# Transpose copies of batch 0's queries exchanged between ScalarE and VectorE, and batch 1's second query transposed three matmuls later

One NeuronCore of one Trainium2 chip. The metric is the device time of one execution in microseconds (us), smaller is better.

## The reference

Linear attention over 8 batches, 8 heads, 576 positions of 64 features, followed by a gated feed-forward block over all 4608 tokens:

```python
q_s = exp(q - max(q, -1));  q_s = q_s / (sum(q_s, -1) + 1e-09)       # per position
k_s = exp(k - max(k, 2));   k_s = k_s / (sum(k_s, 2) + 1e-09)        # per feature
kv  = einsum('bhsd,bhse->bhde', k_s, v)
x   = einsum('bhsd,bhde->bhse', q_s, kv)     # then (b, s, h*d): 4608 x 512
g   = x @ w_gate                             # 512 -> 1536
out = (g * sigmoid(g) * (x @ w_val)) @ w_out # 1536 -> 512
```

## The kernel before

The feed-forward block fills TensorE for nearly the whole run; the attention of each batch is threaded in between. A batch has two groups G of four heads. For each, the query goes: exponential (`eq`, ScalarE), row sums and product with their reciprocals (`qs`, VectorE), nine 128x128 transposes on TensorE into two PSUM banks (`tp`), and a copy of each bank to SBUF (`qt`). The keys and values give `kv` on TensorE, which is normalised to `kn`; the product of `kn` and `qt` is `xp`, copied to `xt`, the feed-forward's input. From batch 2 on, the transposes run on the DMA queues; the change touches batches 0 and 1 alone.

```python
BANKS = ((0, 5), (5, T))                 # T = 9 blocks: 640 and 512 columns

def turn_pe(b, G, i):                    # transposes of one bank
    ...
    tp = s["tp", i] = psp.tile([128, 1024], BF16, tag="ps", name="tp")
    for t in range(t0, t1):
        nc.tensor.transpose(out=tp[...], in_=s["qs"][:, t, :], identity=ident)

def turn_out(b, G, i, eng):              # copy of one bank to qt, on eng
    ...
# ---- batch 0 (cut)
turn_out(0, 0, 0, nc.scalar)
exp_of("k", 0, 1)
turn_out(0, 0, 1, nc.scalar)
norm_mul(0, 1, BANKS)                    # qs of query 1, VectorE
spin(6)
kv_first(0)
key_sum(1)
scale_first(0, nc.scalar)                # kn of group 0
turn_pe(0, 1, 0)
turn_pe(0, 1, 1)
turn_out(0, 1, 0, nc.vector)
turn_out(0, 1, 1, nc.vector)
xp0 = x_mm(0, 0, 0), x_mm(0, 0, 1)       # the first product
kv_first(1, *BANKS[0])
kv_first(1, *BANKS[1])
x_out(0, 0, 0, xp0[0], (nc.scalar, None))
scale_first(1, nc.vector)                # kn of group 1: half ScalarE, half VectorE
x_out(0, 0, 0, xp0[0], (None, nc.vector))
x_out(0, 0, 1, xp0[1])
xp1 = x_mm(0, 1, 0), x_mm(0, 1, 1)       # the second product
# ---- batch 1 (cut); o_mm(j, ..., m0, m1) are output matmuls of row block j
i = norm_mul(1, 1)                       # qs of the second query, VectorE
cast_v(1, 0)                             # v to bf16, GpSimd
c = cast_v(1, 1)
...
o_mm(2, p2, m0=4)                        # eight matmuls
turn_out(1, 0, 1, nc.vector)
turn_pe(1, 1, 0)                         # the second transposes
turn_pe(1, 1, 1)
turn_out(1, 1, 0, nc.scalar)
turn_out(1, 1, 1, nc.vector)
st["kv", 1] = [bank("kv") for _ in range(2)]
p3 = o_mm(3, m1=6)                       # six matmuls
o_out(2, p2)
kv_both(1)
scale_both(1)                            # kn
exp_of("q", 2, 0)
o_mm(3, p3, m0=6, m1=11)                 # five, while kn is made
x_and_next_kv(1, with_kv=False)          # the product of batch 1
o_mm(3, p3, m0=11)                       # one, while xt is copied
```

The softmax here doesn't subtract the row's maximum and nothing guards it: scores larger than these inputs give would overflow.

## Time and profile before

| | before |
|---|---|
| time, median of 3 runs first, of 6 with those beside the changed kernel | 311.65, then 311.62 (311.32 to 311.97) |
| span in the profile | 309.74 |
| first output matmul | 37.755 |
| from there to kv of batch 1 | 10.363 |
| from there to the last TensorE instruction | 267.968 |

Three-decimal times are starts of single instructions, read from the trace in narrow windows. The page's shares and TensorE's waits stand in the prediction. The following rows are the timeline of the kernel before (start, duration, engine, line, operation, what it writes from what, shapes, count, and in brackets the idle time before it with what is taken to have ended it):

```profile
12.70 0.44 PE L202 MATMUL xp<-qt,kn 64*64 64x320 bf16 x8
...
13.47 0.31 ACT L420 ACTIVATE kn<-kv,kvr 128x64 bf16<-128x64 f32 x1
13.52 0.28 DVE L424 TENSOR_SCALAR kn<-kv,kvr 128x64 bf16<-128x64 f32 x1
...
13.84 0.45 PE L202 MATMUL xp<-qt,kn 64*64 64x320 bf16 x8 [0.42 <-DVE kn L424]
...
42.20 2.01 POOL L124 CAST vb<-v 128x1152 bf16<-128x1152 f32 x1 [20.27 <-DMA v<-in_v_dram]
44.80 1.36 DVE L149 TENSOR_TENSOR qs<-eq,rr 128x1152 bf16<-128x1152 bf16 x1
...
47.42 0.67 ACT L108 COPY qt<-tp 128x640 bf16<-128x640 bf16 x1
...
48.12 0.69 PEld L189 LDWEIGHTS <-ek 64*64 64x64 bf16 x72 [0.42 <-ACT qt L108]
```

### The profile page before, as it was taken

The page shows a single profiled execution, that of the slowest core. Times are in us where ns is not written, and L with a number is a line of the kernel's source. Part 1 is how long each engine was busy: PE and PEld are TensorE (multiplying, and loading weights), DVE is VectorE, ACT ScalarE, POOL GpSimd, SP SyncE. Part 2 cuts the span into 40 slices and gives each one's busy share as a digit, 9 for nine tenths or more (in the row PEclk, how much of TensorE's full clock was granted, in tenths as well). Part 3 has the DMA queues.
Part 4 walks back from the last instruction along what each step waited for, and adds up shares of the span by engine and source line. Part 5 has one row for each costly group of instructions (what it writes and reads, how often), then busy time and mean ns, then how long its engine had stood idle before and what let it go on. Part 6 is the DMA issues. An engine that isn't in the chain of part 4 may idle for free.

```text
span 309.7 us, 5467 instructions
## 1 busy us (share of the span) xinstructions
PE 302.8 (98%) x2182; PEld 150.3 (49%) x2182; DVE 161.9 (52%) x286; ACT 146.3 (47%) x214; POOL 32.8 (11%) x39
## 2 busy tenths in 40 slices
PE   6999999999999999999999999999999999999995
PEld 2688745554445444454445444544444444444443
DVE  3844477945754566365826492639353324433421
ACT  5843578785674375547464737455043113312300
POOL 2960021510200110002000200000000000000000
PEclk9999999999999999999999999999999999999999
DMA  7999999999347815590739352605310302020133
GB/s 273 189 195 207 275 389 389 349 219 389 79 87 200 327 33 114 135 382 13 144 74 353 102 121 61 186 0 107 72 35 0 70 11 56 3 68 8 26 71 103
DMA packets 43018, 45.78 MB, mean 148 GB/s; under 512 B 19568, under 2 KB 28272, under 8 KB 42992
## 3 DMA queue, kind: packets, MB, share of 16 engines
q1 hardware_dynamic: 34096, 39.95, 43.4%
q0 software_dynamic: 8752, 5.31, 12.0%
q8 instruction: 17, 0.28, 0.4%
q10 hardware_dynamic: 144, 0.16, 0.2%
q14 instruction: 9, 0.07, 0.1%
HBM read 37.75 MB, written 9.44 MB: 152 GB/s over the span
## 4 chain that ended last, share of the span: by engine, by line
PE 96%; DMA 1%; DVE 0%; ACT 0%; issue 0%
PE g_ps L284 30%; PE u_ps L284 30%; PE o_ps L317 29%; PE kv L189 2%; PE xp L245 1%; PE idle L388 1%; DMA q<-in_q_dram 1%; PE tp L164 1%; PE o_ps L338 1%; DVE rs L135 0%; PE xp L202 0%; PE kv L411 0%; ACT eq L121 0%; ACT xt L259 0%; PE ks L397 0%; DVE o_sb L342 0%
## 5 line engine op out<-in xcount | busy, mean ns | idle before, releaser
L291 ACT ACTIVATE sg<-g_ps 128x512 bf16<-128x512 f32 (+2 forms) x120 | 64.7, 554 | 133.6 <-PE g_ps L284 120.5
L293 DVE TENSOR_TENSOR hr<-sg,u_ps 128x512 bf16<-128x512 bf16 (+3 forms) x120 | 72.5, 616 | 86.3 <-PE u_ps L284 80.7
L284 PE MATMUL g_ps<-xt,wg 128*128 128x512 bf16 (+2 forms) x480 | 111.4, 358 | 0.1
L284 PE MATMUL u_ps<-xt,wv 128*128 128x512 bf16 (+2 forms) x480 | 111.3, 358 | 0.0
L317 PE MATMUL o_ps<-wo,hr 128*128 128x512 bf16 x420 | 93.9, 379 | 0.0
L284 PEld LDWEIGHTS <-wv 128*128 128x128 bf16 x480 | 46.9, 98 | 46.4
L284 PEld LDWEIGHTS <-wg 128*128 128x128 bf16 x480 | 46.3, 98 | 45.5 <-issue 0.6
L317 PEld LDWEIGHTS <-hr 128*128 128x128 bf16 x420 | 40.9, 98 | 48.6
L110 DVE COPY o_sb<-o_ps 128x512 f32<-128x512 f32 x33 | 22.4, 680 | 39.0 <-PE o_ps L317 39.0
L124 POOL CAST vb<-v 128x1152 bf16<-128x1152 f32 x14 | 17.8, 1277 | 135.8 <-DMA v<-in_v_dram 106.6
L135 DVE TENSOR_REDUCE rs<-eq 128x18 f32<-128x1152 bf16 (+2 forms) x18 | 21.7, 1213 | 12.7 <-ACT eq L121 12.7
L149 DVE TENSOR_TENSOR qs<-eq,rr 128x1152 bf16<-128x1152 bf16 (+2 forms) x18 | 22.1, 1234 | 0.1
L121 ACT ACTIVATE eq<-q 128x1152 bf16<-128x1152 f32 (+2 forms) x18 | 18.3, 1051 | 4.1 <-DMA q<-in_q_dram 4.0
L121 ACT ACTIVATE ek<-k 128x1152 bf16<-128x1152 f32 (+2 forms) x17 | 17.9, 1101 | 0.5 <-DMA k<-in_k_dram 0.5
L291 ACT ACT_TABLE_LOAD x12 | 15.4, 1283 | 0.2
L121 ACT ACT_TABLE_LOAD x11 | 14.1, 1283 | 0.2
L388 PE MATMUL idle<-zero 128*128 128x512 bf16 x20 | 7.9, 560 | 2.6 <-DVE rs L135 1.4
L259 ACT CAST xt<-xp 128x512 bf16<-128x512 f32 x14 | 7.8, 586 | 4.5 <-PE xp L245 4.5
L260 DVE CAST xt<-xp 128x512 bf16<-128x512 f32 x14 | 9.0, 683 | 0.7 <-PE xp L245 0.7
L189 PEld LDWEIGHTS <-ek 64*64 64x64 bf16 x504 | 6.3, 107 | 1.7 <-ACT qt L108 0.4
L189 PE MATMUL kv<-vb,ek 64*64 64x65 bf16 x504 | 6.7, 194 | 0.0
L245 PE MATMUL xp<-qt,kn 64*64 64x512 bf16 (+1 forms) x112 | 6.7, 292 | 0.0
(44 smaller groups left out, 67.4 us busy)
## 6 DMA issues: line engine op xcount, KB each, us to landing
q<-in_q_dram SPq DMA_DIRECT2D x16, 576.0 KB, 5.4
out_dram<-o_sb SPq DMA_DIRECT2D x70, 128.0 KB, 2.3
k<-in_k_dram SPq DMA_DIRECT2D x12, 576.0 KB, 7.2
v<-in_v_dram SPq DMA_DIRECT2D x12, 576.0 KB, 9.1
wo<-in_moe_w_out_dram POOLq DMA_DIRECT2D x4, 384.0 KB, 15.4
k<-in_k_dram SPq DMA_DIRECT2D x4, 320.0 KB, 8.2
k<-in_k_dram SPq DMA_DIRECT2D x4, 256.0 KB, 8.1
v<-in_v_dram SPq DMA_DIRECT2D x2, 320.0 KB, 6.9
```

The source lines that it names most:

```text
L110: eng.tensor_copy(out=out, in_=in_)
L121: nc.scalar.activation(out=e[:, t0:t1], in_=src[:, t0:t1], func=AF.Exp)
L124: return nc.gpsimd.tensor_copy(out=vbs[G][:, :, :, 0:64], in_=raw["v", b, G].rearrange("p h (t d) -> p t h d", d=64),)
L135: i = nc.vector.reduce_sum(out=rs[:, 2 * t0:2 * t1], in_=eq2[:, 2 * t0:2 * t1, :], axis=mybir.AxisListType.X)
L149: last = eng.tensor_mul(qs[:, t0:t1, :].rearrange("p t (h d) -> p (t h) d", d=64), eq2[:, 2 * t0:2 * t1, :], s["rr"][:, 2 * t0:2 * t1].to_ ...
L189: nc.tensor.matmul(out=kv[g][HALF[h], c:c + 65], lhsT=ek[HALF[g], t, h, :], rhs=vbs[G][HALF[g], t, h, :], start=(t == 0), stop=(t == T - 1),)
L245: nc.tensor.matmul(out=o[h][HALF[g], c:c + 64 * (t1 - t0)], lhsT=kn[HALF[h], g, G, :], rhs=qt[G][HALF[h], t0:t1, 64 * g:64 * g + 64], star ...
L284: nc.tensor.matmul(out=gu[a][i][:, 0:w_], lhsT=(wg, wv)[a][:, kk, ms], rhs=xt[:, kk, c:c + w_], start=(kk == 0), stop=(kk == KT - 1),)
L291: nc.scalar.activation(out=sg[:, 0:w_], in_=g_ps[:, 0:w_], func=AF.Silu)
L293: nc.vector.tensor_mul(hr[:, m, r:r + w1], sg[:, 0:w1], u_ps[:, 0:w1])
L317: nc.tensor.matmul(out=o_ps, lhsT=hr[:, m, r0:r0 + 128], rhs=wo[:, m, :], start=(m == 0), stop=(m == MT - 1),)
L388: i = nc.tensor.matmul(out=idle, lhsT=zero[:, 0:128], rhs=zero, start=True, stop=True)
```

## The change

The intent is to take a copy off ScalarE where kn of group 0 follows, to free VectorE's xp copy from waiting behind kn, and to keep TensorE busy while VectorE makes qs of batch 1's second query.

```diff
+    def turn_bank(b, G, i):
+        st[b, G]["tp", i] = psp.tile([128, 1024], BF16, tag="ps", name="tp")
     def turn_pe(b, G, i):
...
-        tp = s["tp", i] = psp.tile([128, 1024], BF16, tag="ps", name="tp")
+        if ("tp", i) not in s:
+            turn_bank(b, G, i)
+        tp = s["tp", i]
@@ batch 0
-        turn_out(0, 0, 1, nc.scalar)
         norm_mul(0, 1, BANKS)
+        turn_out(0, 0, 1, nc.vector)
...
-        turn_out(0, 1, 0, nc.vector)
+        turn_out(0, 1, 0, nc.scalar)
         turn_out(0, 1, 1, nc.vector)
...
-        x_out(0, 0, 0, xp0[0], (nc.scalar, None))
+        x_out(0, 0, 0, xp0[0])
         scale_first(1, nc.vector)
-        x_out(0, 0, 0, xp0[0], (None, nc.vector))
@@ batch 1
         turn_out(1, 0, 1, nc.vector)
+        for i in range(2):
+            turn_bank(1, 1, i)
+        st["kv", 1] = [bank("kv") for _ in range(2)]
+        p3 = o_mm(3, m1=3)
         turn_pe(1, 1, 0)
         turn_pe(1, 1, 1)
         turn_out(1, 1, 0, nc.scalar)
         turn_out(1, 1, 1, nc.vector)
-        st["kv", 1] = [bank("kv") for _ in range(2)]
-        p3 = o_mm(3, m1=6)
+        o_mm(3, p3, m0=3, m1=6)
```

## The prediction

> **What bounds the kernel now.** I read the page's busy shares first, then the chain that ended last, then TensorE's waits by window, and last the timeline of the two stretches that the change touches: the opening (0 to 17 us) and batch 1's attention between two feed-forward stages (42 to 60 us).
>
> From the page of the kernel before, the busy shares and the chain by line:
>
> ```profile
> PE 302.8 (98%) x2182; PEld 150.3 (49%) x2182; DVE 161.9 (52%) x286; ACT 146.3 (47%) x214; POOL 32.8 (11%) x39
> PE 96%; DMA 1%; DVE 0%; ACT 0%; issue 0%
> ```
>
> TensorE (PE) is the bound: 98% busy and 96% of the chain. VectorE (DVE) and ScalarE (ACT) are half idle, so moving a copy between them is worth only what it lets TensorE do sooner. What can be won is TensorE's idle time in the two stretches. Its waits from 0 to 17 us, complete:
>
> ```profile
> PE idle L388 <- DVE rs L135: 1.4, 1, 1.4
> PE idle L388 <- DVE sel L367: 1.2, 1, 1.2
> PE xp L202 <- DVE kn L424: 0.4, 1, 0.4
> ```
>
> The first two are start-up (loads, softmax sums) and untouched. The third is the wait of batch 0's second product (xp) for the normalised kv (kn). From 42 to 60 us the same view lists no wait at all, but that is an effect of modelled matmul ends. The weight-load row shows what the matmul row hides:
>
> ```profile
> 44.25 1.45 PEld L317 LDWEIGHTS <-hr 128*128 128x128 bf16 x8
> 46.21 0.17 PEld L164 LDWEIGHTS <-qs 128*128 128x128 bf16 x3 [0.52 <-DVE qs L149]
> ```
>
> The weights of batch 1's second transposes could not be loaded before the normalised query qs was written. The matmul rows around it:
>
> ```profile
> 44.30 1.89 PE L317 MATMUL o_ps<-wo,hr 128*128 128x512 bf16 x8
> 46.22 0.28 PE L164 MATMUL tp<-ident,qs 128*128 128x128 bf16 x2
> ```
>
> The eight output matmuls start 216 ns apart, the last at 45.81; TensorE is free for the next at 45.81 + 0.22 = 46.03. The transposes start at 46.22, just after qs is done (VectorE's product runs 44.80 to 46.16). So TensorE stands idle 46.22 - 46.03 = 0.19 us here. The 0.52 in brackets is not the stall: the weight loader always runs ahead and rests while the array streams.
>
> **What the Trainium skill says.** "TensorE: Matmul & The Clock Gate", section "Wait — 56ns, not 53.3ns?", gives 55.6 and 215.7 ns start to start for 128 and 512 columns at full clock. The trace agrees: 24 output matmuls hold the chain 5.18 us (216 ns each) and nine transposes plus the hand-over take 46.22 to 46.73 (57 ns each). "TensorEngine Tiling (Array Packing)", section "Key Properties", says that a change of tiling mode drains TensorE. The trace agrees with a gap: before the first 64x64 kv matmul at 48.12 the last output matmul (start 47.81) has been streamed at 48.03, so 0.09 us are lost; the same 0.08 appears at 58.78, 68.70 and 99.24. This matters, because the profile puts the gap at 48.12 down to ScalarE's copy of qt, which happens to end at 48.10; kv does not read qt, so I take that label for a coincidence. "ScalarE: Activation LUTs", section "What ACT_TABLE_LOAD costs", gives 186 ns + 0.833 ns per element for an ACTIVATE without pointer operands and an overlap of about 93 ns between neighbours: an estimate of 719 ns for 640 columns. The trace has 692 for that copy out of PSUM, so I use the trace. VectorE does the same 640-column bf16 copy in 491 ns and the 512-column one in 415, against ScalarE's 576.
>
> **Part A, the exchange in batch 0.** It takes two copies from one engine and puts them on the other: qt of query 0, second piece (512 columns), goes from ScalarE (576 ns) to VectorE (415); qt of query 1, first piece (640), goes from VectorE (491) to ScalarE (692). VectorE's copy of the first xp bank is put ahead of its kn, and no longer behind. TensorE's order is the same, so I follow each of its waits.
>
> First product (12.70): its last transpose starts at 12.55, ends its stream at 12.61, plus the mode change 0.09 makes 12.70. TensorE itself sets it. kn of query 0 is ready at 12.51 and the earlier qt piece will be ready at about 12.22 on VectorE (behind the product that ends at 11.88). Gain 0.
>
> Second product (13.84): kv of query 1 ends at 13.43. ScalarE's kn half runs 13.475 to 13.79, VectorE's 13.52 to 13.80, and TensorE starts 0.04 later. Now both halves have a copy in front:
> - ScalarE: the 640-column copy starts at 12.585 (when the fifth transpose is done, as VectorE's did), and gives way after 0.59 (its spacing in the trace from 9.784 to 10.372), at 13.17, to the first xp copy, which ran at 13.07 before. That one gives way after 0.32, at 13.495: kn 13.495 to 13.81, 0.02 later than before.
> - VectorE: the 512-column copy starts when the last transpose is done, 12.77 + 0.04 = 12.81, and gives way 0.33 later at 13.14; the xp copy of 320 columns then holds it for 0.40 (13.719 to 14.117 in the trace): 13.53. kn could start there, or some 0.05 later if its pointer operand again costs what lies between 13.43 + 0.04 and 13.52. So 13.53 to 13.59 against 13.52: 0.01 to 0.07 later.
> The second product slips by 0.02 to 0.07; I take 0.04. The xp copies that follow on VectorE come some 0.2 us earlier, but the first feed-forward matmuls, spaced 0.49 per four (2 x 320 + 2 x 256 columns), show no wait for them before, so that buys nothing. Part A: +0.04 us.
>
> **Part B, the later transposes in batch 1.** It moves three of the six output matmuls (m 0 to 2 of row block 3) from behind the nine transposes to ahead of them; no instruction is added. They fill the hole: start at 46.03 in place of 46.73, 3 x 0.216 = 0.65 later, at 46.68, the transposes start, and qs has been ready since 46.16. The hole of 0.19 closes. Then nine transposes 0.51 (47.19), three output matmuls 0.65 (47.84), mode change 0.09: kv at 47.93 in place of 48.12.
>
> Does anything stop kv from starting at 47.93? Its ek halves end on ScalarE at 46.37 and 47.52, its v casts on GpSimd at 47.37. The qt copies: VectorE's is set by the last transpose, 47.34 + 0.04 to 47.81 (0.45 later than before); ScalarE's starts at 47.43 behind the exponentials as before and ends at 48.10. The product that reads them comes at 50.04, or 49.85 now. VectorE must then empty row block 2 (0.68, to about 48.41) before it turns to kn at about 48.78. All have room. The hole before the first feed-forward matmul (streamed 50.88, start 51.13, waiting for ScalarE's xt copy) moves as a whole. Later, ScalarE works behind TensorE until about 59 us, yet the first banks needed again (at 57.2 and 57.9) were read by about 57.2; the transposes by DMA land at 67.2 and 68.2 for use at 68.70 and 69.25. 0.19 us fits. Part B: -0.19 us, which carries to the end, for TensorE shows no wait after 60 us.
>
> **Sum:** -0.19 + 0.04 = -0.15 us: 311.65 - 0.15 = 311.5.
>
> **Rivals.** (1) kv really waits for the qt copy on ScalarE, as the label at 48.12 says. Then kv stays at 48.12, part B gives 0 and the time is 311.7. For it: the label, and 48.10 + 0.03. Against: the data, and the same gap where no such copy runs. (2) kn becomes the bound in the opening: if VectorE can start kn only when the xp copy in front has ended (13.62), the second product slips by 0.15 to 0.2 and eats part B: 311.65. Against: the VectorE rows overlap by 0.08 throughout. (3) The exchange frees the opening: the copy that left ScalarE (11.44 to 12.02) lay right ahead of kn of query 0 (11.98), and an earlier kn would lead to 311.3. Against: kv ends only at 11.94, and TensorE's own transposes set 12.70. (4) Eight PSUM banks are handed out in order of release; the exchange changes that order, and a matmul could draw a bank that is read later. A wait of 0.2 to 0.5 would give 311.8 to 312.
>
> **Range and chances.** Every term is below 0.1% of the time; even both real holes together (0.42 + 0.19) are 0.6 us, and 2% is 6.2 us. The range holds rivals 1 to 3 and the smaller waits of rival 4, and the spread of the runs (0.22 us) with some more for another chip: 311.1 to 311.9. Faster or slower by over 2% could come only from something that no view shows: 0.005 each.
>
> **What would show it.** Right: three output matmuls ahead of the second transposes, whose weight loads wait for no VectorE product; kv of batch 1 0.15 to 0.19 earlier counted from the first output matmul at about 37.8; the second product of batch 0 at 13.85 to 13.91. Wrong: kv still just behind ScalarE's qt copy; a second product at 14.0 or later, or before 13.8; a new PE wait after 52 us.

## The result

The changed kernel takes 311.5 us (median of 6 runs, 311.21 to 311.76) against 311.62 for the kernel before in the same rounds (6 runs, 311.32 to 311.97). The ratio of the mean times of the runs of the same rounds is 0.9996, 95% interval 0.9983 to 1.0009; such ratios are of means of shared rounds, so not quite the ratio of the medians quoted. The times alone do not show even the sign. The traces show more.

From the page of the changed kernel, busy shares and chain:

```profile
PE 299.9 (97%) x2157; PEld 149.6 (48%) x2182; DVE 161.6 (52%) x286; ACT 146.4 (47%) x214; POOL 32.6 (11%) x39
PE 94%; DMA 2%; DVE 1%; issue 1%; ACT 1%; SPq 0%
```

The lower PE share is no loss of work: 2157 in place of 2182 matmul records, with 2182 weight loads in both, are missing records. TensorE's waits from 0 to 17 us in the changed kernel:

```profile
PE idle L393 <- DVE rs L135: 1.7, 1, 1.7
PE idle L393 <- DVE sel L372: 1.2, 1, 1.2
PE kv L416 <- DMA v<-in_v_dram: 0.7, 1, 0.7
PE xp L207 <- ACT kn L425: 0.4, 1, 0.4
PE tp L169 <- DVE qs L149: 0.2, 1, 0.2
```

The wait for kn is as long as before, and two others are there that belong to this execution's loads. The timeline of the changed kernel, the rows that answer to those of before:

```profile
12.63 0.44 PE L207 MATMUL xp<-qt,kn 64*64 64x320 bf16 x8
...
13.40 0.31 ACT L425 ACTIVATE kn<-kv,kvr 128x64 bf16<-128x64 f32 x1
13.47 0.28 DVE L429 TENSOR_SCALAR kn<-kv,kvr 128x64 bf16<-128x64 f32 x1
...
13.77 0.47 PE L207 MATMUL xp<-qt,kn 64*64 64x320 bf16 x8 [0.42 <-ACT kn L425]
...
44.29 2.54 PE L322 MATMUL o_ps<-wo,hr 128*128 128x512 bf16 x11
46.45 0.70 PEld L169 LDWEIGHTS <-qs 128*128 128x128 bf16 x9
46.67 0.67 PE L169 MATMUL tp<-ident,qs 128*128 128x128 bf16 x9
...
47.56 0.67 ACT L108 COPY qt<-tp 128x640 bf16<-128x640 bf16 x1
...
47.91 0.80 PE L194 MATMUL kv<-vb,ek 64*64 64x65 bf16 x72
```

Eleven output matmuls now run without a break where eight stood, the weight loads of the transposes wait for nothing, and kv starts at 47.909 while ScalarE's qt copy is still running (to 48.230). So kv never waited for that copy.

Where the 0.25 us between the two spans went (309.74 to 309.49): the first output matmul comes 0.009 us earlier (37.746), the stretch from it to kv of batch 1 is 0.200 shorter (10.163), from the first output matmul to the last TensorE instruction 0.207 shorter (267.761), and the end after it 0.036 shorter (3.980). All of the stretch's gain is made between 45.8 and 47.9 us, and it reaches the end whole. The opening, with the exchange, gave nothing that can be seen: first to second product 1.142 us before, 1.141 after.

### The profile page after: what moved, and what is told of

It reads as the page before. It is cut to its first block, busy times and chain, and to the rows that moved or that the text cites. A ratio compares the mean times of both kernels' runs of the same rounds, so it can differ in the third digit from the quotient of the medians.

```text
span 309.5 us, 5442 instructions
## 1 busy us (share of the span) xinstructions
PE 299.9 (97%) x2157; PEld 149.6 (48%) x2182; DVE 161.6 (52%) x286; ACT 146.4 (47%) x214; POOL 32.6 (11%) x39
## 4 chain that ended last, share of the span: by engine, by line
PE 94%; DMA 2%; DVE 1%; issue 1%; ACT 1%; SPq 0%
PE g_ps L289 30%; PE u_ps L289 30%; PE o_ps L322 29%; DMA q<-in_q_dram 2%; PE kv L194 2%; PE xp L250 1%; PE o_ps L343 1%; DVE qs L149 0%; DVE rs L135 0%; PE tp L169 0%; SPq L77 0%; PE xp L207 0%; ACT eq L121 0%; ACT xt L264 0%; DVE o_sb L347 0%
## 5 line engine op out<-in xcount | busy, mean ns | idle before, releaser
L322 PE MATMUL o_ps<-wo,hr 128*128 128x512 bf16 x403 | 92.5, 379 | 1.0 <-issue 0.2
L393 PE MATMUL idle<-zero 128*128 128x512 bf16 x20 | 6.4, 474 | 2.9 <-DVE rs L135 1.7
```

The source lines that it names most:

```text
L322: nc.tensor.matmul(out=o_ps, lhsT=hr[:, m, r0:r0 + 128], rhs=wo[:, m, :], start=(m == 0), stop=(m == MT - 1),)
```

## The experiments

Twelve kernels were run, all with correct results. A "hole" is the start of the first of batch 1's second transposes, less the start of the matmul before it, less 0.216. Times are from the profiles; "out" is the first output matmul.

| kernel | out at | xp to xp | hole | out to kv | out to last PE |
|---|---|---|---|---|---|
| before | 37.755 | 1.142 | 0.190 | 10.363 | 267.968 |
| changed | 37.746 | 1.141 | 0 | 10.163 | 267.761 |
| e1 exchange alone | 37.870 | 1.182 | 0.116 | 10.288 | 267.890 |
| e2 later alone | 37.963 | 1.142 | 0 | 10.162 | 267.764 |
| e3 one matmul | 37.741 | 1.142 | 0 | 10.163 | 267.768 |
| e4 six matmuls | 37.577 | 1.142 | 0 | 10.164 | 267.818 |
| e5 large hole | 38.042 | 1.892 | 0.981 | 11.155 | 268.760 |
| e6 ScalarE loaded | 38.382 | 1.660 | 0.051 | 10.226 | 267.824 |
| e7 kn ahead of copy | 37.900 | 1.174 | 0.071 | 10.455 | 268.091 |
| e8 kv ahead | 38.059 | reordered | 0 | 10.163 | 267.770 |
| e9 VectorE pause | 37.515 | 1.287 | 0.427 | 10.601 | 268.200 |
| e10 cast after product | 37.503 | 1.142 | 0.067 | 10.501 | 268.098 |
| e11 kn filled | 37.885 | 1.142 | 0.069 | 10.565 | 268.090 |
| e12 both fills | 37.740 | 1.142 | 0 | 10.164 | 267.637 |

The theory was the prediction's: the hole is all of the gain, the exchange is worth nothing or a little less. The rivals: the exchange gained; kv waits for the copy; the hole is absorbed later.

**e1, the exchange alone.** The changed kernel with batch 1 as before (the last hunk of the diff undone).

> The exchange of copies alone (part A), batch 1 as before. My theory: it is worth nothing. First to second product of batch 0 (xp to xp on TensorE) 1.14 to 1.16 us, as in both kernels (1.142 before, 1.141 after); the hole before batch 1's second transposes is still there (last output matmul to first transpose 0.41 us, of which 0.19 is idle); kv of batch 1 is 10.36 us after the first output matmul, as before (after: 10.16); span within 0.2 of 309.7. Rival (the exchange is what gained): kv-to-output distance does not matter, the first output matmul comes 0.15 us or more before 37.75 and the span is 309.5 or less.

One run, 311.61 (before on the same chip 311.72). The hole is still there, as the weight-load row of e1's timeline says:

```profile
46.25 0.51 PEld L164 LDWEIGHTS <-qs 128*128 128x128 bf16 x9 [0.44 <-DVE qs L149]
```

The first output matmul is 0.115 later than before, not earlier, so nothing of the rival is seen. That start alone would not exclude it, because it varied by 0.54 us under one and the same opening (see the end of the next section). But in all thirteen profiles with this order the first product starts 0.148 to 0.150 after the last transpose: TensorE itself sets it, and an earlier kn of query 0 cannot move it. Two things missed. First to second product took 1.182, because the second piece of v landed at 13.194, after TensorE had come to kv (its first half began at 13.043); in the profile before it landed at 12.946 with no wait. And the hole is 0.116 and not 0.190. The reason is in the loads as well: in the profile before, batch 1's query landed at 38.938 and ScalarE's exponential started only then (38.960, 1.205 after the first output matmul); in e1 it landed at 38.867, before ScalarE was ready, and the exponential started 1.135 after. 0.116 is the hole when the load is in time, and a late load adds to it.

**e2, the later transposes alone.** The changed kernel with the hunks of batch 0 undone.

> The later transposes alone (part B), copies of batch 0 as before. My theory: the whole of the gain. Last output matmul ahead of the transposes to the next PE work 0.22 us (no hole), kv of batch 1 10.16 us after the first output matmul (before 10.36), second product of batch 0 1.14 us after the first; from the first output matmul to the last matmul of the trace 267.76 us (before 267.97, after 267.76). Rival (both parts are needed, since the other bank order lets part B work): kv at 10.36.

One run, 311.59 (before 311.72). All four numbers came out: no hole, kv at 10.162, 1.142, 267.764. With the copies as before, the whole of the gain is there. It is there although batch 1's query was late: ScalarE's exponential started 1.374 after the first output matmul, and qs was 0.24 later than in e1.

**e3 and e4, one matmul and six.**

```diff
-        p3 = o_mm(3, m1=3)
+        p3 = o_mm(3, m1=1)        # e3;   e4: m1=6, and the second call left out
...
-        o_mm(3, p3, m0=3, m1=6)
+        o_mm(3, p3, m0=1, m1=6)
```

> As the changed kernel, but one output matmul in place of three goes ahead of the second transposes. My theory: the hole is 0.19 us and one matmul is 0.216, so one fills it: transposes about 0.22 us later than TensorE came free, at least 0.08 us after qs was done, kv of batch 1 at 10.16 us after the first output matmul, same as with three. Rival (the transposes need more distance from qs, or the three are what hides the copies): kv 10.2 to 10.36.

> As the changed kernel, but all six output matmuls go ahead of the second transposes. My theory: kv itself does not wait for the qt copies, so kv stays at 10.16 us after the first output matmul; but VectorE's copy of qt now starts only 0.65 us later, its emptying of row block 2 after it ends near 49.0, so kn starts some 0.25 us later than in the changed kernel and the product of batch 1 comes 12.25 to 12.35 us after the first output matmul (changed kernel 12.08, before 12.28): the gain is lost at kn. Rival (kv waits for ScalarE's qt copy, as the profile's label says): kv itself at 10.6 or later.

e3: 311.36, kv at 10.163; the transposes started at 46.229, qs was done at 46.070. One matmul of 0.216 us closed the hole as well as three. e4: 311.27, kv again at 10.164, while ScalarE's qt copy ran from 47.625 to 48.317 and kv started at 47.741: the rival is refuted a second time. But my expectation for the product failed: it came at 12.084, not 12.25 or later. VectorE's kn was late, by 0.185 (its second half was done 12.100 us after the first output matmul, in the changed kernel 11.915), yet the first two matmuls of the product need only the first half of kn, done at 11.697, and what sets them is TensorE's own work: in every profile with five matmuls in between the product starts 1.919 to 1.921 after kv. The lateness shows one step further on: the next two start 0.070 behind them (49.731 after 49.661; 0.006 in the changed kernel), and 267.818 is 0.057 more than with three. So six is too many, by 0.06 us, and three is no better than one in these two profiles. Where the query is late it should be: in e2 the hole would have been 0.116 + 0.24 = 0.36, of which one matmul leaves 0.14 by this sum (an estimate, not run).

**e5, the hole enlarged.**

```diff
-        o_mm(2, p2, m0=4)
+        o_mm(2, p2, m0=4, m1=8)
...
-        p3 = o_mm(3, m1=3)
         turn_pe(1, 1, 0)
         turn_pe(1, 1, 1)
+        o_mm(2, p2, m0=8)
+        p3 = o_mm(3, m1=3)
```

> The reverse of part B, enlarged: batch 1's second transposes stand four output matmuls earlier than in the kernel before, so TensorE must wait for qs longer. My theory: the hole grows from 0.19 by 4 x 0.216 = 0.86 to 1.05 us, and all of it reaches the end, for nothing behind it has slack: kv 11.2 us after the first output matmul (before 10.36), time 0.8 to 0.9 us over the kernel before, 312.5, ratio 1.0027. Rival (a hole there is taken up later by waits that shrink): less than 0.4 us at the end.

312.53 (4 runs, 312.0 to 314.67) against 311.86 (7 runs, 311.26 to 312.62), ratio 1.0035, interval 0.9996 to 1.0074: the right size, too wide to be proof. The trace is the proof:

```profile
44.59 1.03 PE L322 MATMUL o_ps<-wo,hr 128*128 128x512 bf16 x4
46.43 0.68 PE L169 MATMUL tp<-ident,qs 128*128 128x128 bf16 x9 [0.82 <-DVE qs L149]
```

The hole is 0.981, which is e1's 0.116 plus four times 0.216. From the first output matmul to the last TensorE instruction it took 268.760, which is 0.870 over e1's 267.890: a hole here reaches the end whole. (The 1.892 from product to product in e5, and e9's 1.287, are waits for the second piece of v, which landed at 13.199 and 12.656; they lie ahead of the first output matmul and are not in these intervals.) The run of 314.67 has no profile and stays unexplained.

**e6, both copies of query 1 on ScalarE.** `turn_out(0, 1, 1, nc.scalar)` in place of `nc.vector`.

> The changed kernel with both qt copies of batch 0's second query on ScalarE. My theory: ScalarE's half of kn then starts only behind the two copies and the first xp copy, near 13.98 in the times of the kernel before: first to second product 1.6 to 1.65 us in place of 1.14, and about 0.45 us at the end: ratio to before 1.0008 (part B gives back 0.2). Rival (the placement of these copies has slack on both engines): 1.14 to 1.2.

311.93 (4 runs) against 311.86, ratio 0.9997, interval 0.9974 to 1.002: the times decide nothing. The trace gives 1.660 between the products, as expected, and TensorE's wait for kn doubled. e6's waits of TensorE, then its ScalarE timeline:

```profile
PE xp L207 <- ACT kn L425: 0.9, 1, 0.9
```

```profile
12.70 1.18 ACT L108 COPY qt<-tp 128x640 bf16<-128x640 bf16 x2
13.77 0.44 ACT L108 CAST xt<-xp 128x320 bf16<-128x320 f32 x1
14.09 0.34 ACT L425 ACTIVATE kn<-kv,kvr 128x64 bf16<-128x64 f32 x1
```

VectorE's half of kn was done at 13.921 here, ScalarE's at 14.427, and the product started at 14.479. That 0.052 is the key to the exchange: in all thirteen profiles with the product in this order it starts 0.052 to 0.054 after ScalarE's half ends. ScalarE's half sets it, also in the profile before, where the label names VectorE's. The source says why: the first two matmuls of the product read `kn[:, 0]`, which ScalarE writes, and the next two `kn[:, 1]`, which VectorE writes. The trace has both waits apart: in all profiles but e6 and e7, where VectorE's half was done early enough, the third matmul starts 0.054 to 0.056 after VectorE's half ends. A late VectorE half delays this pair alone (0.034 behind the first matmul in the changed kernel, 0.017 before, 0.007 in e7), and the fifth matmul still comes 0.160 after the first in all thirteen.

**e7, kn ahead of VectorE's xp copy**, the order of before, with the exchange kept.

> The changed kernel, but VectorE's kn goes ahead of its first xp copy again, as in the kernel before. My theory: VectorE's kn then starts 0.05 to 0.1 us after kv ends, not when the copy gives way (0.12), and TensorE's second product follows ScalarE's half: 1.11 to 1.14 us after the first; no change at the first output matmul beyond 0.05 us. Rival (the order at VectorE costs what part A lacks): 1.05 or less and the first output matmul 0.1 us earlier.

311.83 (before 311.86). VectorE's kn started 0.094 after kv ended, as in the kernel before (0.093), against 0.121 in the changed kernel. So the copy in front costs VectorE's half 0.03 us, which does not reach the product's start. The product came 1.174 after the first, not 1.14: ScalarE's chain of qt copy (12.707), xp copy (13.296) and kn (13.614) was back to back here, its kn 0.065 after kv in place of 0.049 and 0.332 long in place of 0.313. The rival (1.05) is excluded. Not expected was the 10.455 further down; e11 tells why.

**e8, the second kv ahead of the first product.**

```diff
-        xp0 = x_mm(0, 0, 0), x_mm(0, 0, 1)
         kv_first(1, *BANKS[0])
         kv_first(1, *BANKS[1])
-        x_out(0, 0, 0, xp0[0])
+        xp0 = x_mm(0, 0, 0), x_mm(0, 0, 1)
         scale_first(1, nc.vector)
+        x_out(0, 0, 0, xp0[0])
```

> The changed kernel with batch 0's second kv put ahead of the first product, and both kn halves ahead of the xp copies, so that the product fills TensorE's wait for kn. My theory: the second product and the first feed-forward matmul come 0.2 to 0.3 us earlier, but the gain dies on the way to the first output matmul, because slices of the weights land 0.04 to 0.15 us before they are used in the traces of both kernels (uses at 20.99 and 24.91 before, landings 20.88 and 24.76): new weight-load waits for DMA between 17 and 30 us, first output matmul at most 0.12 us earlier than 37.75. Rival (the opening has no other limit than kn): first output matmul 0.2 us or more earlier, at 37.55 or before.

311.69 (before 311.86). No gain, but the limit was another one than I named. e8's TensorE timeline:

```profile
12.72 0.35 PE L416 MATMUL kv<-v,ek 64*64 64x64 bf16 x20
13.43 0.32 PE L416 MATMUL kv<-v,ek 64*64 64x64 bf16 x16 [0.35 <-DMA v<-in_v_dram]
```

kv came earlier only to wait for the second piece of v, which landed at 13.384; the first output matmul came at 38.059. The weights set no new wait in this profile. So in e8, as in e1, the opening is paced by a load of v, and rearranging engines cannot show a gain there. That the weights are close behind is seen elsewhere. In the changed kernel one slice landed at 17.110, and the matmul that needs it started at 17.156, 0.037 later than the spacing of its neighbours asks for. From the first feed-forward matmul to the first output matmul it took 23.577 there, 23.586 in e10, 23.699 in e5 and 23.716 in e9, with matmuls that start 0.046 after a slice lands, against 23.530 to 23.537 in the other ten profiles. Whether they would have eaten e8's gain had v been in time stays open.

**e9, a pause on VectorE**, in the kernel before: a memset of 432 fp32 ahead of the first query's product. e10 and e11 belong with it:

```diff
-        norm_mul(1, 0)                       # e10: i0 = norm_mul(1, 0)
-        cast_v(1, 0)
+        c0 = cast_v(1, 0)                    # e10, on the changed kernel
+        tc.add_manual_dep(c0.ins, i0.ins.name, SYNC, reason="order of the vector port")
...
-        o_mm(3, p3, m0=6, m1=11)
+        o_mm(3, p3, m0=6, m1=10)             # e11, on the changed kernel
         x_and_next_kv(1, with_kv=False)
-        o_mm(3, p3, m0=11)
+        o_mm(3, p3, m0=10)
```

> The kernel before with one VectorE memset of 432 fp32 (0.45 us) put in front of the product that makes batch 1's first qs, so that this product starts after GpSimd's first cast of v in place of ahead of it. My theory (from two earlier runs, where the cast began first and the product took 1.95 and 2.17 us in place of 1.36): the product loses to the cast and takes 1.9 to 2.3 us, so qs of the second query is late by 0.45 plus 0.5 to 0.9 us and the hole before the second transposes is 1.1 to 1.6 us; if v happens to land late, so that the product is first again, 1.36 us and a hole of 0.55 to 0.65. Rival (VectorE's long products in those runs have another cause): 1.36 us although the cast started first, hole 0.55 to 0.65.

> The changed kernel with GpSimd's first cast of v in batch 1 made to wait for VectorE's product of the first query. My theory: the product takes 1.36 us in the profile, the cast starts just behind it and takes 1.15, kv of batch 1 comes 10.16 us after the first output matmul, as in the undisturbed profiles, span as in the changed kernel and no run over 312.2. Rival (the long products have another cause, or the cast was needed earlier): a product over 1.5 us, or kv later than 10.2.

> The changed kernel with one of the five output matmuls between batch 1's kv and its product moved to behind the product, where TensorE waits for ScalarE's xt copy. My theory: the product then starts when kn is ready, 0.12 to 0.16 us earlier (11.93 to 11.96 us after the first output matmul in place of 12.08), and all that follows moves with it: first to last TensorE work 267.60 to 267.65 in place of 267.76; time 0.13 us under the changed kernel, which the rounds alone will hardly show. Rival (the wait for xt moves nowhere): 267.76.

The question behind e9 and e10 came from e6 and e7: the product that makes batch 1's first qs took 1.95 and 2.17 us there and 1.36 elsewhere. e9 did not create the case: the pause delayed the product by 0.34 only and v landed so that the product was first again (311.56; product 1.29, hole 0.427, less than the 0.55 expected). It tells nothing of the theory, and it shows once more that VectorE's lateness opens the hole one for one (0.427 is 0.116 plus 0.31, by which qs was later). But e11 fell into the case by itself. Its timeline, GpSimd and VectorE, and then e10's:

```profile
41.83 1.14 POOL L124 CAST vb<-v 128x1152 bf16<-128x1152 f32 x1 [20.28 <-DMA v<-in_v_dram]
...
41.90 2.28 DVE L149 TENSOR_TENSOR qs<-eq,rr 128x1152 bf16<-128x1152 bf16 x1
```

```profile
43.81 1.14 POOL L124 CAST vb<-v 128x1152 bf16<-128x1152 f32 x1 [21.97 <-DVE qs L149]
...
42.38 1.36 DVE L149 TENSOR_TENSOR qs<-eq,rr 128x1152 bf16<-128x1152 bf16 x1
```

Against them the row of GpSimd in the kernel before (42.20, 2.01 long, behind a product that started at 41.84). "SBUF — State Buffer" of the Trainium skill, section "Who interferes with whom", says that a VectorE instruction with two SBUF inputs and a GpSimd instruction that reads SBUF contend for a port pair that is an exclusive lock; its section "Summary: rules for kernel authors" says that the second one to issue "fully blocks" until the first finishes. Every profile agrees, but for some 0.15 us by which winner and loser overlap. Where the cast started first (e6, e7, e11) the product ended 1.208, 1.209 and 1.208 us after the cast's end; where the product started first (before, changed, e1 to e5, e8, e9) the cast ended 1.002 to 1.009 after the product's end.

Which of them is first depends on when v lands. When the product loses, qs of the second query is 0.6 to 0.9 us later against the first output matmul (8.91 in e6, 9.14 in e7 and 9.25 in e11, 8.33 undisturbed), the first transposes are late too in e7 and e11 (by 0.20 and 0.31, not in e6), and a hole of 0.05 to 0.07 is left even behind three moved matmuls. One matmul would leave 0.43 more there, by the sum; it was not run.

e10: 311.36 (4 runs, 311.27 to 311.48) against 311.64 (11 runs, 311.19 to 312.52), ratio 0.9987, interval 0.9972 to 1.0003. The cast ran behind the product, but kv came at 10.501, since batch 1's query landed only at 39.473, 1.97 us after an early first output matmul. The guard does not help against that, and this profile does not test it: v landed at 42.723, after the product had started (42.378), so the product would have been first in any case. e11: 311.35 (6 runs) against the same 311.64, ratio 0.9989, interval 0.9975 to 1.0003. From kv to the product it took 1.704 in place of 1.920, so the edit works, but the blocked product put it behind, and 267.76 was not reached.

**e12, both edits.**

> The last two edits together. My theory: their effects add: product at 11.93 to 11.96 us and kv at 10.16 us after the first output matmul in the profile, first output matmul to last TensorE work 267.60 to 267.65, no long VectorE product, median 311.1 to 311.6 and ratio to the kernel before 0.998 to 1.000. Rival: a guard that delays kv, 10.2 or more.

311.42 (6 runs, 310.82 to 312.02) against 311.64, ratio 0.9991, interval 0.9974 to 1.0008. In its profile kv is at 10.164 and the last TensorE instruction at 267.637, 0.124 under the changed kernel, inside what was expected. Here too v landed (42.236) after the product's start (41.930), so the guard stays untested, and the gain is that of the other edit. e12's TensorE timeline:

```profile
48.64 1.04 PE L322 MATMUL o_ps<-wo,hr 128*128 128x512 bf16 x4
49.61 0.78 PE L250 MATMUL xp<-qt,kn 64*64 64x512 bf16 x16
50.32 0.60 PE L322 MATMUL o_ps<-wo,hr 128*128 128x512 bf16 x2
50.78 0.54 PE L289 MATMUL g_ps<-xt,wg 128*128 128x448 bf16 x2
```

The product began 11.868 us after the first output matmul, earlier than the 11.93 expected, because its first half waits for half of kn alone, as in e4; the second pair then waited 0.10. e12 has the shortest stretch of all, and no timing separates it from the changed kernel.

## Why the prediction was right

Time, range and the mechanism of part B held in full; part A was mis-sized by 0.04 us and rests on other facts than I gave. The drain at a change of tiling mode, which the prediction put at 0.09 and 0.08, is 0.093 to 0.094 at every change of the kernel before; no sum turns on that.

1. *TensorE is idle for 0.19 us before the second transposes, and this is all that part B can win.* Shown: the hole is gone, kv is 0.200 earlier, and 0.207 of it arrives at the end. e2 has it without the exchange, e1 lacks it, and e5 shows that a hole of 0.98 arrives whole. But I took 0.19 for a property of the program. It is 0.116 when batch 1's query lands in time (e1), 0.07 more in the profile that I read because it landed late, and by the sum larger again when GpSimd blocks VectorE. The term is a number of one execution, and its agreement with the measured 0.200 (I had expected 0.15 to 0.19) is no independent check, since both come from the same profile of the kernel before. Against e1, whose query was in time, the later transposes are worth 0.125 at kv and 0.129 at the end.
2. *kv does not wait for ScalarE's qt copy (rival 1).* Shown twice: kv starts before the copy ends in the changed kernel (47.909 against 48.230) and in e4.
3. *The exchange costs 0.02 to 0.07 us; I took 0.04.* Measured: 0.00 in the profiles where v is not late (1.141 or 1.142 in the changed kernel, e3, e4, e10, e11, e12). Two steps failed. The first is the choice of VectorE's half of kn as what sets the product. It did slip by 0.03, as worked out, but the product's start waits for ScalarE's half alone. The second is the start of ScalarE's qt copy, which I took to be 0.115 ahead of the first product (12.585 against 12.70). In these profiles it was over 0.3 ahead and out of the way, because VectorE's qs was late there against TensorE: the transposes paused between the fifth and the sixth (12.009 and 12.302 in the changed kernel), so the first bank was full early. The changed kernel, then e7:

```profile
11.79 0.91 PE L169 MATMUL tp<-ident,qs 128*128 128x128 bf16 x9
...
12.27 0.69 ACT L108 COPY qt<-tp 128x640 bf16<-128x640 bf16 x1
```

```profile
12.23 0.66 PE L169 MATMUL tp<-ident,qs 128*128 128x128 bf16 x9
...
12.71 0.69 ACT L108 COPY qt<-tp 128x640 bf16<-128x640 bf16 x1
```

In e7 the transposes ran without a pause, the copy started 0.117 ahead, and ScalarE's half ended 0.034 and the second product 0.032 later against the first than before, within what I had worked out. So the exchange costs 0.00 to 0.03 us, by how early qs is against TensorE. The second product at 13.770 missed the expected 13.85 to 13.91 and even met one of my signs of being wrong ("before 13.8"). That sign was badly made: the whole opening was 0.07 earlier, and only the distance between the products says anything of the exchange.

4. *kn becoming the bound (rival 2), a freed opening (rival 3).* Neither is seen. Rival 2's late VectorE half would delay only the second pair of matmuls; rival 3 falls because the last transpose sets the first product in all thirteen profiles, as said under e1. e8 adds that an earlier kv would wait for v.
5. *Banks handed out otherwise (rival 4).* The exchange did deal them differently (in the built programs the first two output blocks use banks 0 and 3 in place of 3 and 2), and no wait of TensorE for a bank is seen in the trace.

What stays open is the time itself. The sum of -0.15 agrees with the medians' -0.12, but the kernel before alone spread from 311.19 to 312.62 over its 25 runs, so that agreement proves nothing; the trace's -0.20 is the evidence. With the same opening, the first output matmul came anywhere from 37.503 to 38.042 (changed, e1, e3 to e5, e10 to e12), more than either part of the change is worth. I suspect the blocked product behind some of the slower runs of the kernel before, where an estimate from e7 (qs 0.81 later against the first output matmul, the first transposes 0.2 later themselves) makes the hole about 0.7 in place of 0.12; no run over 312.1 of it was profiled, so this is not shown.

## What to carry to other kernels

A hole on the bounding engine is worth its length and no more, so measure it from the last start plus one matmul's spacing (here 0.216 us), not from the idle times in the bracket, and fill it with independent work of at least that length; a little more guards against executions in which the producer is late, as e2's was. Moving work between two engines that are both half idle is worth nothing until one shows which of them sets the next start: look in the source for what the first instruction reads, and in several traces for the constant gap (here 0.052 to 0.054 us after ScalarE, in thirteen profiles), rather than at the label. When the expected gain is a tenth of the spread of the runs, decide by intervals inside the trace, and expect each to carry the landing times of one execution.

## What the Trainium skill lacked or had wrong

- "TensorEngine Tiling (Array Packing)", section "Key Properties", has a drain at a change of tiling mode but no figure: beyond the spacing of the matmul ahead of it, it cost 0.093 to 0.094 us at each of the eleven changes from 128x128 to 64x64 in the trace of the kernel before.
- "SBUF — State Buffer", section "Who interferes with whom", is right on the lock; it has no figure for this pair. VectorE's product of 1152 columns takes 1.36 us alone and up to 2.28 behind a GpSimd cast of the same size; the cast takes 1.14 alone and up to 2.32 behind the product (2.01 in the kernel before).
- "ScalarE: Activation LUTs", section "What ACT_TABLE_LOAD costs", has figures for an ACTIVATE with immediate operands, from which one gets estimates of 719 ns for 640 columns and 612 for 512; it has none for the copies out of PSUM here, which the traces list as COPY and show at 692 (671 at another place) and 576.
- No page that I read has a figure for the time from the end of an instruction on another engine to the start of a matmul that waited for its result: here 0.052 to 0.054 us after ScalarE and 0.054 to 0.056 after VectorE at the products, and 0.057 to 0.059 after VectorE at the second transposes of the eight profiles with a hole.
